# Loading the first query and key blocks of two batches as 2 KB rows and the first weight tiles as fp32 on the same queue, and moving one batch's transposes to DMA

## The chip, the cores and the metric

The kernel runs on one core of one Trainium2 chip. The metric is the device time of one execution, in microseconds (us). Times are medians of several runs. The kernel before the change took 301.33 us (three runs, 300.98 to 301.36). A run counts as slow when it is more than 1.5% above the fastest of its kernel. A point is one per cent of the time before.

## The reference

Two parts follow one another. The first is a sparse attention over 4 batches, 8 heads, 768 tokens and 64 features. Each query picks the 6 best of the 24 chunks of 32 keys by an upper bound, and attends only to these. The second is a gated feed-forward network over the 3072 tokens.

```python
k_min, k_max = min and max of k over each chunk of 32 tokens
ub = np.sum(np.maximum(q * k_min, q * k_max), axis=-1)        # one bound per query and chunk, causal
top_chunks = np.argsort(ub, axis=-1)[..., -6:]
scores = scale * np.matmul(q, k.transpose(0, 1, 3, 2))        # masked to chosen chunks and causal
attn = softmax(scores)
x = (attn @ v) as [3072, 512]                                 # tokens x (heads * features)
gate = np.maximum(x @ w_gate, 0.0)                            # w_gate, w_val: 512 x 1536
out = (gate * (x @ w_val)) @ w_out                            # w_out: 1536 x 512
```

## The kernel before

The first 128 tokens of each batch see only four chunks, so they need no selection. They are done first, as four "first blocks" (one a batch). The other tokens are 16 attention jobs: 4 batches times 4 pairs of heads, job 0 to 3 being batch 0. The feed-forward network runs in six units of 512 tokens and fills TensorE between the attention jobs.

The order of instructions on each engine is not written by hand. Each operation is given to a static list scheduler, called the plan, with an engine, an expected cost in us, a priority (lower goes first) and the things it needs and makes. The plan simulates the kernel from these numbers and fixes one order for each engine. So an edit of a cost or of one load moves many other instructions too.

All plain loads, all transposes that DMA does and all stores are issued by SP, one after the other, in the plan's order. Loads that cast fp32 to bf16 on the way are issued by GpSimd, on another queue.

The loads of a first block, one for each batch and each of q, k, v (256 KB, rows of 64 floats, so 256 bytes):

```python
    def first_block(b):
        ...
                nc.sync.dma_start(out=t[:, 0:H * D].rearrange("p (h d) -> p h d", d=D),
                                  in_=src[b, :, 0:128].rearrange("h p d -> p h d"))
        ...  # then: GpSimd casts to bf16, TensorE transposes, ACT or DVE copies, TensorE scores
```

A transpose is TensorE's or DMA's, by a switch for each batch:

```python
    PE_KQ = lambda b: b < 2          # keys and queries of batches 0 and 1: TensorE
    PE_X = lambda b: b < 2           # attention output of batches 0 and 1: TensorE
    ...
        if on_pe:
            ... nc.tensor.matmul(t[:, r, :], s[:, r, :], ident[0:np_, 0:np_], is_transpose=True, ...)
        else:
            ... nc.sync.dma_start_transpose(out=t, in_=src())
```

The weights come by casting loads from GpSimd, in groups of 2, 3, 3 and 4 column tiles, and a number places the feed-forward work against the jobs:

```python
    WGS = [2, 3, 3, 4]
    ...
                nc.gpsimd.dma_start(out=o, in_=i)          # fp32 in DRAM, bf16 on chip
    ...
            p = 4.0 + HP * (u + done / total)              # priority of feed-forward unit u
```

The softmax here doesn't subtract the row's maximum and nothing guards it: scores larger than these inputs give would overflow.

Of the kernel before, what the change touches and what calls it, by code (L numbers as in the profile page):

```python
# [14 lines left out]
BF16 = mybir.dt.bfloat16  # L15
# [9 lines left out]
class Plan:  # L25
# [8 lines left out]

    LAG = {"PE": 0.38, "ACT": 0.06, "DVE": 0.06, "POOL": 0.06, "SP": 0.06, "DMA": 1.5, "SDMA": 1.7}

    def __init__(self, rings, banks):
        self.rings = rings
        self.banks = banks
        self.ops = []  # L40
        self.made = defaultdict(list)
        self.users = defaultdict(int)
        self.big = set()
# [16 lines left out]
    def share(self, flow, t, events):  # L60

        for s in flow.values():
# [4 lines left out]
            (0.35, 0.65) if flow["DMA"][0] in self.big else (0.21, 0.93))  # L67
# [6 lines left out]
    def order(self):  # L74
# [21 lines left out]
        while len(seq) < n:  # L96
# [13 lines left out]
            for i in ends:  # L110
                o = ops[i]
                for name in [x for _, x in o[5]] + list(o[6]):
                    left[name] -= 1
                for d in outs[i]:
                    need[d] -= 1
                    at[d] = max(at[d], t + (o[7] if ops[d][0] != o[0] else 0.0))
                    if need[d] == 0:
                        wait[ops[d][0]].append(d)
                        heapq.heappush(events, (at[d], -1))
# [40 lines left out]
def kernel(  # L160
# [51 lines left out]
    WIDE = lambda b: b < 1  # L212
    WS = 8
# [3 lines left out]
    PE_KQ = lambda b: b < 2  # L217
    PE_SEL = lambda b: b < 1
    PE_X = lambda b: b < 2
# [5 lines left out]
    WGS = [2, 3, 3, 4]  # L225
# [46 lines left out]
    for nm in "kq":  # L272
        TAGS[f"{nm}bf"] = ([128, 1024], BF16, 2)
        TAGS[f"{nm}0"] = ([128, 512], BF16, 2)
# [15 lines left out]
    rings["dq"] = 6  # L290
    rings["xT"] = XU
    plan = Plan(rings, set(PS))
# [58 lines left out]
    def free_half(j):  # L351
        b, hp = JOBS[j]
        for h in range(2):
# [3 lines left out]
               after=["ind"] + ([("s", j - HP)] if b else []), makes=[("kx0", hp)])  # L357


    def turned(name, tag, src, nr, on_pe, prio, after, makes, hold, np_=128):  # L360
# [10 lines left out]
        else:  # L371
# [3 lines left out]
            dma_t(nr, prio, f, after, makes, take=[(tag, name)], hold=hold)  # L375
# [4 lines left out]
    def dma_t(nr, prio, f, after, makes, take=(), hold=()):  # L380

        made = makes[0]
        op("SP", 1.25, prio, f, after=after, makes=[("ti", made)], take=take, hold=hold, lag=0.0)
        op("DMA", 0.144 * nr, prio, None, after=[("ti", made)], makes=makes,
           hold=list(hold) + [x for _, x in take])
# [18 lines left out]
    def first_block(b):  # L404
        p0 = -30.0 + b
        src3 = (("k", k), ("q", q), ("v", v))
        for nm, src in src3:
            rn = (nm + "raw", "P", b)

            def f_ld(nm=nm, src=src, rn=rn):  # L410
                t = new(nm + "raw", rn)
                nc.sync.dma_start(out=t[:, 0:H * D].rearrange("p (h d) -> p h d", d=D),
                                  in_=src[b, :, 0:128].rearrange("h p d -> p h d"))
            op("SP", 0.6, -40.0 + b + (1.5 if nm == "v" else 0.0), f_ld, makes=[("iss", nm, b - B)],
               take=[(nm + "raw", rn)] + [("dq", ("dq", nm, b - B, i)) for i in range(2)], lag=0.0)
            op("DMA", 1.22, -40.0 + b + (1.5 if nm == "v" else 0.0), None, after=[("iss", nm, b - B)],
               makes=[("ld", nm, b - B)],
               hold=[rn] + [("dq", nm, b - B, i) for i in range(2)])
            if nm == "v":
                op("POOL", 0.61, p0 - 0.1, lambda rn=rn: nc.gpsimd.tensor_copy(  # L420
                    out=v0_l[b % 2][:, :, 0:D],
                    in_=TL[rn][:, 0:H * D].rearrange("p (h d) -> p h d", d=D)),
                    after=[("ld", nm, b - B), ("v00", b % 2), ("av0", b - 2)],
                    makes=[("v", "P", b)], hold=[rn])
                continue
            bn = (nm + "bf", "P", b)

            def f_cast(nm=nm, rn=rn, bn=bn):
                nc.gpsimd.tensor_copy(out=new(nm + "bf", bn)[:, 0:H * D],
                                      in_=TL[rn][:, 0:H * D])  # L430
            op("POOL", 0.61, p0 - 0.2, f_cast, after=[("ld", nm, b - B)], makes=[bn],
               take=[(nm + "bf", bn)], hold=[rn])
            tn, cn = (nm + "T", "P", b), (nm + "0", b)
            tT = turned(tn, "F", lambda bn=bn: TL[bn][:, 0:H * D].rearrange(
                "p (i x) -> p i x", x=128), HP, True, p0, [bn], [tn], [bn])

            def f_c(nm=nm, tT=tT, cn=cn):
                o = new(nm + "0", cn)
                if nm == "q":
                    nc.scalar.activation(out=o, in_=tT(), func=ACT.Copy)  # L440
                else:
                    nc.vector.tensor_copy(out=o, in_=tT())
            op("ACT" if nm == "q" else "DVE", 0.6 if nm == "q" else 0.43, p0, f_c, after=[tn],
               makes=[cn], take=[(nm + "0", cn)], hold=[tn])
        kn, qn, sn, an, xn = ("k0", b), ("q0", b), ("sT", "P", b), ("aT", "P", b), ("x", "P", b)

        def f_s():
            t = new("S", sn)
            for h in range(2):
                nc.tensor.matmul(t[:, h], ident, tri.unsqueeze(1).to_broadcast([128, HP, 128]),  # L450
                                 start=True, stop=False)
            for i in range(HP):
                cs = slice(128 * i, 128 * i + 128)
                for h in range(2):
                    hs = slice(64 * h, 64 * h + 64)
                    nc.tensor.matmul(t[:, h, cs], TL[kn][hs, cs], TL[qn][hs, cs], start=False,
                                     stop=(i == HP - 1))
        op("PE", 0.85, p0, f_s, after=[kn, qn, "tri", "ident"], makes=[sn], take=[("S", sn)],
           hold=[kn, qn])

# [37 lines left out]
    def job_front(j):  # L498
# [4 lines left out]
        wide = WIDE(b)  # L503
# [3 lines left out]
        for nm, src in (("k", k), ("q", q), ("v", v)):  # L507
            rn = (nm + "raw", j)
            big = wide and nm != "v"
# [6 lines left out]
            def f_ld(nm=nm, src=src, rn=rn, np_=np_, ns=ns, lo=lo, big=big):  # L516
# [6 lines left out]
                else:  # L523
                    nc.sync.dma_start(out=o.rearrange("p (h r d) -> p h r d", h=2, d=D),
                                      in_=s.rearrange("h (r p) d -> p h r d", p=128))
            dq = [("dq", nm, j, i) for i in range({"k": 1, "q": 0}[nm] if big else 3)]
            op("SP", 0.6, pL, f_ld, makes=[("iss", nm, j)],
               after=[("iss", x, -1) for x in "kqv"],
               take=[(nm + "raw", rn)] + [("dq", x) for x in dq], lag=0.0)
            i = op("DMA", n * (0.00137 if big else 0.00234), pL, None, after=[("iss", nm, j)],  # L530
                   makes=[("ld", nm, j)], hold=[rn] + dq)
            if big:
                plan.big.add(i)
# [41 lines left out]
        tok = lambda a: a.rearrange("f (p s) -> f p s", s=WS) if wide else a  # L575
# [8 lines left out]
        for m, o in ((0, ALU.min), (1, ALU.max)):  # L584
            def f_mm(m=m, o=o):
                if m == 0:
                    new("kmm", mm)
                if wide:
# [3 lines left out]
                nc.vector.tensor_reduce(out=TL[mm][:, m], in_=i, axis=AX.XY if wide else AX.X,  # L592
# [5 lines left out]
        if PAIR(b):  # L598
            copy_half("DVE", n, pT + 0.05, tok(kx[0]), kT, None,
                      [kn] + [("s", i) for i in prev], [("kx", j)], [kn])  # L600
        for h in range(0 if PAIR(b) else 2):
            copy_half(eng[h], n, pT + 0.05, tok(kx[h][64 * h:64 * h + 64]), kT, h,
# [17 lines left out]
        for nm, e, o in (("qmn", "ACT" if on_pe else "ACT", -1.0),  # L620
                         ("qmx", "ACT" if on_pe else "DVE", 1.0)):
            def f_q(nm=nm, e=e, o=o):
                t = new(nm, (nm, j))
                if e == "ACT":
                    nc.scalar.activation(out=tok(t), in_=qT(), func=ACT.Relu, scale=o)  # L625
# [5 lines left out]
        if PAIR(b):  # L631
            copy_half("ACT", n, pT + 0.06, tok(qx.rearrange("f r h p -> f (r h p)")[:, 0:SQ]), qT,
                      None, [qn, ("s", j - NQX)], [("qx", j)], [qn])

    def job_sel(j):
# [68 lines left out]
        else:  # L704
            dma_t(2 * NQ, p, lambda: nc.sync.dma_start_transpose(
# [67 lines left out]
    def job_av(j, off):  # L773
# [56 lines left out]
        for pi, rs in enumerate(parts):  # L830
# [15 lines left out]
            else:  # L846
                dma_t(len(rs), p, f_xc, aft, mk, take=tk, hold=hd)


    def s1(u, nt, p, wide):  # L850
# [6 lines left out]
        def f_mm(m):  # L857
# [7 lines left out]
            for kt in range(KT_):  # L865
                nc.tensor.matmul(ps, w[:, kt, cs], xT[:, kt, xc:xc + 512], start=(kt == 0),  # L866
                                 stop=(kt == KT_ - 1))
        for m, nm in ((0, gn), (1, vn)):
            op("PE", 0.858, p + 0.001 * m, lambda m=m: f_mm(m),
               after=[xn, ("w", gi)] + ([("g0",) + gn] if m and wide else []),  # L870
               makes=[("d",) + nm] + ([] if m else [("g0",) + gn]),
# [125 lines left out]
```

## Time and profile before

| | before |
|---|---|
| median time, us | 301.33 |
| span of the profiled run, us | 300.6 |
| TensorE busy, us | 273.4 |
| TensorE idle in 0 to 60 / 60 to 200 / after 200 us | 16.3 / 6.6 / 4.3 |

The idle times are the length of a stretch minus the busy time in it. These two lines are from the page of the kernel before: busy time by engine (share of the span, number of instructions), and the chain of work that ended last.

```profile
PE 273.4 (91%) x2258; PEld 145.6 (48%) x2292; DVE 168.3 (56%) x482; ACT 162.5 (54%) x222; POOL 98.0 (33%) x186
...
PE 70%; DMA 18%; DVE 5%; issue 2%; POOL 2%; ACT 1%; SPq 0%; POOLq 0%; ACTq 0%; DVEq 0%
```

TensorE is the bound: busy for 91% of the span. 34 matrix instructions of 2292 have no record in this trace, so its busy time is somewhat more than 273.4 us. The next table is the view of stretches of the same kernel: for each stretch (start and end in us), its length, then busy us of each engine, the clock that TensorE was granted (1.00 is full), the mean busy share of the DMA engines (it adds up the time of all packets, so it can exceed 1) and the rate. The clock has no record before it first went full, at 16.3 us here, and the view shows 1.00 for that time too.

```profile
core 0: us, PE busy (x) PEld busy (x) DVE busy (x) ACT busy (x) POOL busy (x), PEclk, DMA share, GB/s
0.00:60.00 60.00, 43.68 (x443) 24.21 (x449) 39.06 (x118) 28.66 (x38) 32.26 (x56) 0.97 1.20 213
60.00:200.00 140.00, 133.40 (x1350) 77.23 (x1367) 103.08 (x325) 104.06 (x135) 65.29 (x129) 1.00 1.01 176
200.00:320.00 120.00, 96.34 (x473) 44.20 (x479) 26.20 (x40) 29.77 (x50) 0.41 (x1) 0.99 0.09 33
```

60 minus 43.68 is the 16.3 us of idle TensorE in the first stretch; 140 minus 133.40 is 6.6. So there is something to be won in the first 60 us, where the DMA engines are full, and little afterwards. The timeline of GpSimd shows when data comes: each line is start, duration, engine, line of the program, operation, output and input, and in brackets the idle time before it and what ended that.

```profile
4.04 0.61 POOL L429 CAST kbf<-kraw 128x512 bf16<-128x512 f32 x1 [0.97 <-DMA kraw<-in_k_dram]
5.22 0.61 POOL L429 CAST qbf<-qraw 128x512 bf16<-128x512 f32 x1 [0.57 <-DMA qraw<-in_q_dram]
6.43 0.61 POOL L429 CAST kbf<-kraw 128x512 bf16<-128x512 f32 x1 [0.59 <-DMA kraw<-in_k_dram]
7.65 0.61 POOL L429 CAST qbf<-qraw 128x512 bf16<-128x512 f32 x1 [0.61 <-DMA qraw<-in_q_dram]
...
23.02 1.04 POOL L550 CAST kbf<-kraw 96x1024 bf16<-96x1024 f32 x1 [2.16 <-DMA kraw<-in_k_dram]
25.59 1.04 POOL L550 CAST kbf<-kraw 96x1024 bf16<-96x1024 f32 x1 [1.54 <-DMA kraw<-in_k_dram]
```

The first casts start 1.2 us apart, and each waited for its load: 256 KB each 1.2 us is 218 GB/s. The last two are the keys of jobs 0 and 1.

Finally, what TensorE waited for from 60 to 200 us (total, times, longest), the largest item:

```profile
PE sT L741 <- DMA qx_93<-cb_97: 1.8, 1, 1.8
```

These are chosen queries, which DMA transposes for the later batches. TensorE's waits are short here.

### The profile page before, as it was taken

Reading aid. Unit: us, or ns where it says so; the run is one execution under the profiler, and the core shown is the slowest. Engines: PE = TensorE matmul, PEld = TensorE weight load, DVE = VectorE, ACT = ScalarE, POOL = GpSimd, SP = SyncE. Lnnn points to the kernel's source line nnn. Section 1 sums busy time; section 2 is a strip of 40 time slices with the busy share of each in tenths; the row PEclk is TensorE's granted clock in tenths of the full one; section 3 lists DMA queues with packets and bytes.
Section 4 is the critical chain, followed back from the end, with each engine's and each line's share of the span. In section 5 each row is a group of like instructions: output and inputs, shape, how many; then the busy total and the mean of one; then the engine's idle time right before and its main releaser. Section 6 shows DMA issues by size and latency. Waiting matters only on the chain.

```text
span 300.6 us, 5925 instructions
## 1 busy us (share of the span) xinstructions
PE 273.4 (91%) x2258; PEld 145.6 (48%) x2292; DVE 168.3 (56%) x482; ACT 162.5 (54%) x222; POOL 98.0 (33%) x186
## 2 busy tenths in 40 slices
PE   2975796998999999989979899999999999999995
PEld 1542343654665655646545555554444444444441
DVE  4456896759987898978759683204343013103310
ACT  3442494497457868878769867463323223323321
POOL 5674345438644556655644321120000000000000
PEclk9999998999999999999999999999999999999999
DMA  9999999999799999999999622322000020020002
GB/s 168 217 249 215 223 223 227 184 213 221 143 237 234 183 221 204 192 206 188 228 215 236 120 46 44 92 81 59 0 0 0 37 105 0 35 107 0 1 37 106
DMA packets 118269, 41.29 MB, mean 137 GB/s; under 512 B 108128, under 2 KB 113760, under 8 KB 118240
## 3 DMA queue, kind: packets, MB, share of 16 engines
q1 hardware_dynamic: 112448, 36.19, 64.0%
q0 software_dynamic: 5792, 4.72, 9.9%
q8 instruction: 18, 0.29, 0.4%
q14 instruction: 11, 0.09, 0.1%
HBM read 31.20 MB, written 6.29 MB: 125 GB/s over the span
## 4 chain that ended last, share of the span: by engine, by line
PE 70%; DMA 18%; DVE 5%; issue 2%; POOL 2%; ACT 1%; SPq 0%; POOLq 0%; ACTq 0%; DVEq 0%
PE g L866 23%; PE yp L901 19%; PE vl L866 9%; PE sT L741 7%; PE o L793 6%; DMA qraw<-in_q_dram 5%; DMA kraw<-in_k_dram 5%; DMA qx_92<-cb_96 3%; DMA qx_91<-cb_95 3%; DMA qx_93<-cb_97 2%; PE sT L731 2%; DVE hT L885 1%; PE kT L367 1%; PE xt L367 1%; PE ub L651 1%
## 5 line engine op out<-in xcount | busy, mean ns | idle before, releaser
L753 ACT ACTIVATE aT<-sT 128x1024 bf16<-128x1024 f32 x80 | 79.6, 1026 | 23.4 <-PE sT L741 15.7
L877 ACT ACTIVATE grl<-g 128x512 bf16<-128x512 f32 x72 | 43.1, 599 | 57.3 <-PE g L866 57.3
L765 POOL TENSOR_SCALAR_AFFINE_SELECT aT<-aT 128x256 bf16<-128x256 bf16 x80 | 32.3, 418 | 55.7 <-ACT aT L753 47.5
L885 DVE TENSOR_TENSOR hT<-vl,grl 128x512 bf16<-128x512 f32 x48 | 33.0, 688 | 25.2 <-PE vl L866 20.6
L901 PEld LDWEIGHTS <-hT 128*128 128x128 bf16 x288 | 27.4, 98 | 30.6
L885 DVE TENSOR_TENSOR hT<-g,grl 128x512 bf16<-128x512 f32 x24 | 16.6, 692 | 45.2 <-ACT grl L877 29.5
L901 PE MATMUL yp<-wo_70,hT 128*128 128x512 bf16 x141 | 34.8, 379 | 0.2
L592 DVE TENSOR_REDUCE kmm<-kT 128x24 bf16<-128x768 bf16 x32 | 29.6, 946 | 9.0 <-PE kT L367 4.5
L901 PE MATMUL yp<-wo_69,hT 128*128 128x512 bf16 x137 | 34.3, 379 | 0.4
L911 ACT ACTIVATE y<-yp 128x512 f32<-128x512 f32 x24 | 14.3, 596 | 35.0 <-PE yp L901 33.5
L793 PEld LDWEIGHTS <-aT 128*128 128x128 bf16 x640 | 23.7, 99 | 8.2 <-POOL aT L765 2.4
L741 PEld LDWEIGHTS <-kx_all 128*128 128x128 bf16 x192 | 16.0, 98 | 17.8 <-DMA qx_91<-cb_95 2.5
L866 PE MATMUL g<-xT,wg_64 128*128 128x512 bf16 x91 | 24.1, 379 | 0.2
L550 POOL CAST kbf<-kraw 128x768 bf16<-128x768 f32 (+1 forms) x16 | 14.4, 898 | 14.1 <-DMA kraw<-in_k_dram 11.5
L866 PE MATMUL g<-xT,wg_63 128*128 128x512 bf16 x71 | 18.3, 379 | 0.2 <-issue 0.2
L866 PE MATMUL g<-xT,wg_62 128*128 128x512 bf16 x70 | 18.2, 379 | 0.1
L801 DVE RECIPROCAL zr<-o 128x5 f32<-128x5 f32 x32 | 6.1, 190 | 20.5 <-PE o L793 20.5
L808 DVE TENSOR_TENSOR x<-o,zr 128x320 bf16<-128x320 f32 x32 | 15.7, 492 | 1.1
L866 PE MATMUL vl<-xT,wv_68 128*128 128x512 bf16 x61 | 16.1, 379 | 0.2
L550 POOL CAST qbf<-qraw 128x640 bf16<-128x640 f32 (+1 forms) x16 | 13.0, 810 | 9.2 <-DMA qraw<-in_q_dram 9.2
L625 ACT ACTIVATE qmn<-qT 128x640 bf16<-128x640 bf16 x16 | 11.5, 722 | 7.2 <-PE qT L367 6.2
L866 PEld LDWEIGHTS <-wg_64 128*128 128x128 bf16 x96 | 8.9, 98 | 10.7 <-issue 1.3
(178 smaller groups left out, 407.5 us busy)
## 6 DMA issues: line engine op xcount, KB each, us to landing
kraw<-in_k_dram SPq DMA_DIRECT2D x16, 384.0 KB, 6.3
vraw<-in_v_dram SPq DMA_DIRECT2D x16, 384.0 KB, 6.1
out_dram<-y SPq DMA_DIRECT2D x24, 256.0 KB, 2.1
qraw<-in_q_dram SPq DMA_DIRECT2D x12, 384.0 KB, 5.0
qraw<-in_q_dram SPq DMA_DIRECT2D x4, 320.0 KB, 12.3
kraw<-in_k_dram SPq DMA_DIRECT2D x4, 256.0 KB, 4.8
qraw<-in_q_dram SPq DMA_DIRECT2D x4, 256.0 KB, 5.0
vraw<-in_v_dram SPq DMA_DIRECT2D x4, 256.0 KB, 5.1
```

Of the source, the lines that this page charges most:

```text
L550: nc.gpsimd.tensor_copy(out=new(nm + "bf", bn)[0:np_, 0:(ns - r0) * 2 * D].rearrange("p (r h d) -> p r h d", h=2, d=D), in_=TL[rn][0:np_, ...
L592: nc.vector.tensor_reduce(out=TL[mm][:, m], in_=i, axis=AX.XY if wide else AX.X, op=o)
L741: nc.tensor.matmul(t[:, h, o:o + m * 128].rearrange("k (r p) -> k r p", p=128), kx[h][:, c * 128:(c + 1) * 128], qx[:, qb - 1:qb - 1 + m, ...
L753: nc.scalar.activation(out=TL[an][:, :, a0:a0 + w], in_=TL[sn][:, :, 0:w], func=ACT.Exp, scale=scale)
L765: nc.gpsimd.affine_select(out=d, in_=d, compare_op=ALU.is_ge, fill=0.0, base=0, channel_multiplier=-1, pattern=[[0, 2], [1, 128]])
L793: nc.tensor.matmul(TL[on][:, r - 1, h - h0, :], TL[an][:, h, o:o + 128], vb[:, h, c, :], start=(i == 0), stop=(i == NP - 1))
L808: nc.vector.tensor_tensor(out=TL[xn][:, :, h0 * D:(h0 + hs) * D].rearrange("p r (h d) -> p r h d", d=D), in0=TL[on][:, :, :, 0:D], in1=TL[ ...
L866: nc.tensor.matmul(ps, w[:, kt, cs], xT[:, kt, xc:xc + 512], start=(kt == 0), stop=(kt == KT_ - 1))
L877: nc.scalar.activation(out=new("grl", rn), in_=g, func=ACT.Relu)
L885: nc.vector.tensor_tensor(out=TL[hn][:, nt, :], in0=vv, in1=TL[rn], op=ALU.mult)
L901: nc.tensor.matmul(TL[pn], TL[hn][:, nt, tl * 128:(tl + 1) * 128], wo_sb[nt // NPG][:, nt % NPG, :], start=(nt == 0), stop=(nt == NTI - 1))
L911: nc.scalar.activation(out=new("y", yn), in_=TL[pn], func=ACT.Copy)
```

## The change

The intent is to have the first data sooner, and to take work from TensorE, the bound. There are four items, numbered as the prediction numbers them:

1. The first blocks of two batches are loaded together. One load brings half the heads of two batches, and each of its 128 rows is 8 tokens, 2 KB (2 KB in place of 256 bytes). The transposed data are put in order by the copy that follows.
2. The two batches are then cast, transposed and scored together, the query casts move from GpSimd to VectorE, and the matmuls that write the causal mask go ahead of the data.
3. The first four column tiles of both weights (2 MB of fp32) come as plain loads on SP's queue and are cast on chip.
4. The transposes of batch 1 (k, q, x) go from TensorE to DMA.

Besides, many numbers of the plan change: costs, rates, the place of the feed-forward work (4.0 to 1.0), the order of the weight groups. The core of the diff:

```diff
-    PE_KQ = lambda b: b < 2
+    PE_KQ = lambda b: b < 1
     PE_SEL = lambda b: b < 1
-    PE_X = lambda b: b < 2
+    PE_X = lambda b: b < 1
...
-    WGS = [2, 3, 3, 4]
+    WGS = [4, 4, 4]
...
+    def first_front(bp):
+        p0 = -30.0 + 2 * bp
+        for nm, src in (("k", k), ("q", q)):
...
+            def f_ld(nm=nm, src=src, rn=rn):
+                t = new(nm + "raw", rn)
+                s = src[2 * bp:2 * bp + 2, :, 0:128].rearrange(
+                    "b (i h) (p s) d -> h (b i) p (s d)", h=2, s=WS)
+                for h in range(2):
+                    nc.sync.dma_start(out=t[:, h * WS * D:(h + 1) * WS * D], in_=s[h])
+            xfer((nm, 2 * bp - B), 1.1, 1.45, 2, pl, f_ld, makes=[("ld", nm, 2 * bp - B)],
+                 take=[(nm + "raw", rn)], big=True)
...
+    def first_weights():
+        engs = iter(("DVE", "ACT", "POOL", "DVE"))
+        n = 128 * WGS[0]
...
+                    nc.sync.dma_start(out=new(tag, rn)[:, 0:2 * n].rearrange(
+                        "p (k n) -> p k n", n=n), in_=i[:, x:x + 2, 0:n])
+                xfer((nm, "W", x), 0.5, 1.45, 2, -36.0 + 0.1 * m, f_ld, makes=[("ld",) + rn],
+                     take=[(tag, rn)], big=True)
...
-            p = 4.0 + HP * (u + done / total)
+            p = 1.0 + HP * (u + done / total)
```

## The prediction

> **What bounds the kernel now.** The page's busy table gives TensorE 273.4 us of a 300.6 us span (91%); VectorE, ScalarE and GpSimd are at 56, 54 and 33%. In the table of stretches, TensorE is idle 16.3 us of the first 60 us, 7 us from 60 to 200 us (mostly for queries transposed by DMA), about 0.6 us from 200 to 280 us, and 3.9 us at the end (last copy and store). So TensorE work bounds it after about 55 us, and arriving data before. The chain of waits up to 43 us is nearly all loads: query 15.8 to 27.2, key 28.6 to 43.2. DMA share is over 1 there at only 205 to 230 GB/s.
>
> **What the change does, costed.**
> 1. First blocks: eight q/k loads of 256 KB in 256-byte rows become four pairs of 256 KB loads in 2 KB rows. In the timeline the old ones land 1.2 us apart (218 GB/s). The Trainium skill ("DMA: Bandwidth & Descriptors", Specifications) asks for 512 bytes or more for line rate and gives about 358 GB/s as the HBM limit of a core; no part of this trace shows 2 KB rows alone. Estimate from these: 1.45 us per 512 KB, so about 5.8 in place of 9.6 us, 4 us of DMA time saved.
> 2. Two batches are cast, transposed and scored at once; half of the casts move from GpSimd to VectorE. The first mask matmuls (1.04 us a pair, slow clock) move ahead of the data, where TensorE is idle.
> 3. The first four column tiles of both weights (2 MB of fp32) come over SP's queue, 2 KB rows, and cost four casts (0.7 to 1.05 us) on three engines. Before, the casting GpSimd loads landed 5 to 20 us after issue; wv_65 held TensorE until 25.2 us, wv_66 until 32.3. They are now 4 MB, not 6 MB, beside the SP loads.
> 4. Batch 1's k, q and x transposes leave TensorE for DMA: 64 transposes (by the order of instructions). A group of six takes 0.51 us against 0.22 for one, so 0.058 us each: 3.7 us. In return some 24 more DMA transposes (about 8 us of DMA time, estimated) fall at 60 to 110 us, where the DMA share is already 0.8 to 1.4.
>
> **On the critical path.** Item 4's 3.7 us counts fully: TensorE is nearly saturated there and feed-forward matmuls fill waits. Of the 4 to 5 us of DMA time from 1 and 3, I expect 3 to 4 us as less TensorE idle before 60 us; part goes to a later first feed-forward matmul (it waits for 2 MB of plain loads, beside the casting queue from about 12 us). From 60 to 200 us I give back about 1 us to later DMA transposes. Sum: 301.3 - 3.7 - 3.5 + 1 = about 295.
>
> Predicted: **295.0 us**, 8 in 10 within 289.5 to 299.5. Faster by over 2%: 0.52; within 2%: 0.46; slower: 0.02.
>
> **What would show it.** TensorE busy about 269 to 270 us. Idle before 60 us about 12 to 13 us, from 16.3. First-block q/k landing about 1.5 us per 512 KB. First feed-forward matmul at 20 to 26 us, then no weight waits over 1 us. Job 0's bound matmuls (29.7 us before) at 26 to 33 us. Idle 60 to 200 us at 7 to 9 us.
>
> **What would make it wrong.** The casting queue starving SP's plain weight loads, so that feed-forward starts after 30 us: no gain there, about 298. Or DMA transposes of batch 1 delaying scores by several us. Conversely, if early feed-forward fills every wait, idle before 60 us falls below 9 us and the time to 290.

## More of the kernel before

The timeline of SP shows how it issues (L521 is a load of keys or queries of batch 0, in long rows; x2 is two loads):

```profile
16.29 0.39 SPq L521 DMA_DIRECT2D kraw<-in_k_dram  x1
...
17.27 11.23 SPq L521 DMA_DIRECT2D qraw<-in_q_dram  x2
```

Of these 11.23 us for two issues one took 10.6, and a load of values later took 11.6. SP was then not waiting for data; it stood in the issue itself, while earlier transfers were still being worked off. What stands behind such a load in SP's order waits with it.

## The result, and the profile after

| | before | after |
|---|---|---|
| median time, us (four runs each, same chip) | 301.35 | 317.97 |
| lowest to highest | 300.98 to 302.06 | 316.26 to 318.40 |
| TensorE busy, us | 273.4 | 278.5 |
| TensorE idle in 0 to 60 / 60 to 200 / after 200 us | 16.3 / 6.6 / 4.3 | 21.8 / 11.6 / 3.9 |

The ratio of after to before is 1.0538 (95% interval 1.0493 to 1.0583): slower by more than 5%. A ratio here is the mean time of one kernel's fast runs over the mean of the other's of the same rounds, so it is not quite the ratio of the medians quoted. All ratios below are to the kernel before, run on the same chip in the same rounds.

The page of after, the same two lines:

```profile
PE 278.5 (88%) x2228; PEld 145.1 (46%) x2228; DVE 164.6 (52%) x476; ACT 164.5 (52%) x221; POOL 93.2 (30%) x177
...
PE 44%; DMA 7%; ACT 1%; issue 1%; DVE 0%; POOL 0%; ACTq 0%; POOLq 0%
```

The stretches of after:

```profile
0.00:60.00 60.00, 38.16 (x271) 19.57 (x271) 28.86 (x80) 19.82 (x26) 21.72 (x35) 0.94 0.98 210
60.00:200.00 140.00, 128.36 (x1264) 70.66 (x1263) 101.49 (x318) 96.81 (x127) 63.54 (x122) 0.99 1.10 188
200.00:320.00 120.00, 111.94 (x697) 54.86 (x694) 34.20 (x80) 47.89 (x70) 7.93 (x20) 0.99 0.15 46
```

TensorE's idle time grew by 5.5 us in the first stretch and by 5.0 in the second, and its busy time by 5.1. With 0.4 us less at the end, that accounts for the 15.2 us of span. The growth of busy time is partly a gap in the records of before (34 missing; after has none of its 2228 missing), partly slow clock, as shown further down, so it can't be split exactly. The same gap makes the idle time of before look somewhat longer than it was.

First, when data come. The casts of the key pairs of the first blocks are on GpSimd, and of the query pairs on VectorE; the two later lines of the first fence are the keys of jobs 0 and 1.

```profile
6.45 1.04 POOL L440 CAST kbf<-kraw 128x1024 bf16<-128x1024 f32 x1 [3.39 <-DMA kraw<-in_k_dram]
...
15.35 1.04 POOL L440 CAST kbf<-kraw 128x1024 bf16<-128x1024 f32 x1 [2.15 <-DMA kraw<-in_k_dram]
...
35.96 1.04 POOL L579 CAST kbf<-kraw 96x1024 bf16<-96x1024 f32 x1 [3.33 <-DMA kraw<-in_k_dram]
...
49.22 1.04 POOL L579 CAST kbf<-kraw 96x1024 bf16<-96x1024 f32 x1 [1.67 <-DMA kraw<-in_k_dram]
```

```profile
10.50 0.69 DVE L442 CAST qbf<-qraw 128x1024 bf16<-128x1024 f32 x1 [6.36 <-DMA qraw<-in_q_dram]
...
19.20 0.69 DVE L442 CAST qbf<-qraw 128x1024 bf16<-128x1024 f32 x1 [6.87 <-DMA qraw<-in_q_dram]
```

Before, the last cast of k0, q0, k1 and q1 began at 7.65 us; now the last cast of the same four (one k pair and one q pair) begins at 10.50. The keys of job 0 come at 35.96 in place of 23.02 us, those of job 1 at 49.22 in place of 25.59. What loads did meanwhile is seen in the view of stretches, before and then after:

```profile
4.00:6.00 2.00, 0.72 (x6) 0.46 (x7) 0.57 (x2) 0.00 (x0) 1.22 (x2) 1.00 1.37 219
...
8.00:10.00 2.00, 1.70 (x14) 0.69 (x12) 0.23 (x1) 0.80 (x1) 0.88 (x2) 1.00 1.39 218
```

```profile
4.00:6.00 2.00, 0.98 (x3) 0.07 (x1) 0.15 (x1) 0.00 (x0) 0.00 (x0) 1.00 0.57 212
...
8.00:10.00 2.00, 0.58 (x6) 0.31 (x3) 0.00 (x0) 0.00 (x0) 0.00 (x0) 1.00 0.83 157
```

The DMA engines are not full: their mean share is 0.57 and 0.83 where it was 1.37 and 1.39, and from 8 to 10 us they move 157 GB/s where it was 218. From 4 to 6 us a share of 0.57 moved nearly what 1.37 had moved: long rows do take less engine time for a byte. But part of the engines has nothing to do. Then SP's order in after (L966 loads the fp32 weights, L556 the keys of jobs 0, 1, ...):

```profile
12.49 1.70 SPq L966 DMA_DIRECT2D kraw<-in_moe_w_gate_dram  x1
...
16.03 3.03 SPq L966 DMA_DIRECT2D kraw<-in_moe_w_val_dram  x1
...
21.09 0.41 SPq L556 DMA_DIRECT2D kraw<-in_k_dram  x1
...
24.63 9.99 SPq L556 DMA_DIRECT2D kraw<-in_k_dram  x1
```

The weight loads stand ahead of the keys of job 0 (issued at 21.09, in before from 14.5 us on), and the keys of job 1 stood 10 us in the issue. The first feed-forward matmuls, in TensorE's timeline:

```profile
33.01 1.87 PE L895 MATMUL g<-xT,wg_61 128*128 128x512 bf16 x4 [0.52 <-DVE xT L529]
...
38.05 1.03 PE L895 MATMUL vl<-xT,wv_64 128*128 128x512 bf16 x4
```

Feed-forward begins at 33.0 us (21.5 before), and cold: the same four matmuls take 1.87 us, and 1.03 us from 38.05 on. The clock has its first record, at full, at 38.0 us (16.3 in before). Idle TensorE costs a second time in this way. The stretches around two later gaps show it (the column after POOL's is the clock):

```profile
48.00:51.70 3.70, 1.76 (x16) 0.58 (x13) 1.47 (x2) 0.88 (x2) 1.28 (x2) 0.99 1.19 235
51.70:58.50 6.80, 5.95 (x31) 2.22 (x32) 3.74 (x7) 3.55 (x5) 5.04 (x7) 0.50 0.87 155
120.00:123.30 3.30, 0.78 (x4) 0.41 (x5) 0.41 (x1) 0.97 (x2) 1.06 (x3) 1.00 0.99 172
123.30:126.70 3.40, 3.40 (x21) 1.62 (x19) 0.40 (x1) 1.54 (x2) 0.49 (x2) 0.51 0.84 162
```

After a stretch in which TensorE was busy 1.76 of 3.7 us the clock was half for 6.8 us, and after one with 0.78 of 3.3 us for 3.4 us. Together 10.2 us at half clock, against 3.4 us in before. The Trainium skill ("TensorE: Matmul & The Clock Gate", "Part 1: The HAM clock gate (the "warmup" mystery)", "What's actually happening") says that the clock falls to half after an idle window of about 3.4 us and comes back after as long a busy one. This agrees in the size of the step (0.50 and 0.51 granted) and in the length (3.4 us, and twice that). But TensorE was not wholly idle ahead of either: low use was enough in these two. From 167.7 to 171.1 us it was busy only 1.62 of 3.4 us as well, and the clock stayed full, so where the limit lies is not shown.

From 60 to 200 us the largest wait of TensorE is again for queries transposed by DMA, and longer:

```profile
PE sT L770 <- DMA qx_90<-cb_94: 5.2, 2, 2.7
```

### The profile page after: what moved, and what is told of

It is laid out like the page before. It is cut to its first block, busy times and chain, and to the rows that moved or that the text cites. A ratio compares the mean times of both kernels' runs of the same rounds, so it can differ in the third digit from the quotient of the medians.

```text
span 315.8 us, 5854 instructions
## 1 busy us (share of the span) xinstructions
PE 278.5 (88%) x2228; PEld 145.1 (46%) x2228; DVE 164.6 (52%) x476; ACT 164.5 (52%) x221; POOL 93.2 (30%) x177
## 4 chain that ended last, share of the span: by engine, by line
PE 44%; DMA 7%; ACT 1%; issue 1%; DVE 0%; POOL 0%; ACTq 0%; POOLq 0%
PE g L895 18%; PE yp L932 13%; PE vl L895 6%; DMA kT<-kbf 5%; PE sT L770 4%; PE o L822 2%; DMA qx_90<-cb_94 2%; PE ub L680 0%; ACT aT L782 0%; ACT y L942 0%; POOL aT L794 0%; ACT kx_all L402 0%; DVE hT L916 0%; DVE x L837 0%; DVE zr L830 0%
## 5 line engine op out<-in xcount | busy, mean ns | idle before, releaser
L782 ACT ACTIVATE aT<-sT 128x1024 bf16<-128x1024 f32 x80 | 79.8, 1023 | 23.9 <-PE sT L770 17.1
L932 PE MATMUL yp<-wo_68,hT 128*128 128x512 bf16 x144 | 35.0, 379 | 0.0
L932 PE MATMUL yp<-wo_67,hT 128*128 128x512 bf16 x144 | 35.0, 379 | 0.0
L895 PE MATMUL g<-xT,wg_61 128*128 128x512 bf16 x96 | 26.4, 399 | 0.5 <-DVE xT L529 0.5
L770 PEld LDWEIGHTS <-kx_all 128*128 128x128 bf16 x192 | 16.3, 98 | 22.2 <-DMA qx_90<-cb_94 5.8
L895 PE MATMUL g<-xT,wg_62 128*128 128x512 bf16 x96 | 25.6, 391 | 0.0
L895 PE MATMUL g<-xT,wg_63 128*128 128x512 bf16 x96 | 24.6, 379 | 0.5 <-ACT grl L908 0.5
L895 PE MATMUL vl<-xT,wv_65 128*128 128x512 bf16 x64 | 18.2, 410 | 0.0
L895 PE MATMUL vl<-xT,wv_66 128*128 128x512 bf16 x64 | 16.4, 379 | 1.6 <-DVE hT L916 1.6
L895 PE MATMUL vl<-xT,wv_64 128*128 128x512 bf16 x64 | 17.3, 394 | 0.0
L402 ACT ACTIVATE kx_all<-kT 64x768 bf16<-64x768 bf16 x12 | 10.0, 835 | 11.4 <-DMA kT<-kbf 11.4
L770 PE MATMUL sT<-qx_90,kx_all 128*128 128x512 bf16 (+3 forms) x64 | 11.2, 299 | 5.2 <-DMA qx_90<-cb_94 5.2
```

Source lines behind the costliest of these rows:

```text
L770: nc.tensor.matmul(t[:, h, o:o + m * 128].rearrange("k (r p) -> k r p", p=128), kx[h][:, c * 128:(c + 1) * 128], qx[:, qb - 1:qb - 1 + m, ...
L782: nc.scalar.activation(out=TL[an][:, :, a0:a0 + w], in_=TL[sn][:, :, 0:w], func=ACT.Exp, scale=scale)
L895: nc.tensor.matmul(ps, w[:, kt, cs], xT[:, kt, xc:xc + 512], start=(kt == 0), stop=(kt == KT_ - 1))
L932: nc.tensor.matmul(TL[pn], TL[hn][:, nt, tl * 128:(tl + 1) * 128], wo_sb[nt // NPG][:, nt % NPG, :], start=(nt == 0), stop=(nt == NTI - 1))
```

## The experiments

Eighteen kernels ran. All gave the reference's result but the probe. Where a text names a theory by a letter, the heading or the text beside it says what is tested. Most edits of a kernel also change the plan's order, and the group at the end asks how much that alone is worth. The exception is 8 against 16 engines (after and e2, e3 and e6, e18 and e7): that edit touches only access patterns, and in the traces of all three pairs SP and TensorE have the same operations in the same order.

### A. The eight loads that use eight DMA engines

The Trainium skill ("DMA: Bandwidth & Descriptors", "Why a DMA increments its semaphore by 16 and not by 1") says that a DMA is spread over k engines, where k is the largest number up to 16 that divides the slowest dimension (of a size other than 1) of both its access patterns, and that with loads issued by SP only those k engines post a completion. Here that is 8 for the source (2 batches x 4 heads). The trace agrees: each paired load left 8 completion packets of four bytes, every other load 16. The rival was that the rate of 2 KB rows was simply over-estimated.

**e1_probe**: a kernel of its own (wrong result) loads 256 KB of keys one at a time, each followed by one VectorE instruction that waits for it.

```diff
+ a: k[2*bp:2*bp+2, :, 0:128].rearrange("b (i h) (p s) d -> h (b i) p (s d)", h=2, s=8)   # as in after: slowest 8
+ b: k[2*bp:2*bp+2, :, 0:128].rearrange("b (i h) (p s) d -> h p (b i) (s d)", h=2, s=8)   # same bytes: slowest 16
+ c: k[b, :, 0:128].rearrange("h p d -> p h d")                                           # as before: 256-byte rows, 128
+ d: as a, but each batch by itself: two loads of 128 KB, slowest 4
```

> A probe with a wrong output on purpose: loads of the first blocks one at a time, each waiting for the one before. Theory A (the slowest dimension of the new source pattern is 8, so each new load uses only 8 of the 16 DMA engines): form a (as in the changed kernel, 256 KB, 2 KB rows, slowest dimension 8) takes about 1.3 us longer in data than one with 16 engines would: from the 200 GB/s seen in the changed kernel at 3 to 6 us, 256 KB need 1.3 us, form b (slowest dimension 16, same bytes) about 0.7 us, form d (slowest dimension 4) about 1.3 us as its two halves of 4 engines do not spread either, or 2.6 us if both use the same 4; form c (256-byte rows, 16 engines) 1.2 us. In issue-to-landing time: a 0.6 us above b, a about equal to c. Rival B (the 2 KB rows are fast and the start is slow because of the load of weights on the same queue and beside it): a and b land alike, both well before c.

In the timeline of VectorE, the bracket is the time from the end of the instruction before (when the next load is issued) to the landing; ta to td are the forms a to d.

```profile
9.75 0.69 DVE L37 TENSOR_TENSOR acc<-acc,ta 128x512 f32<-128x512 f32 x1 [4.04 <-DMA ta<-in_k_dram]
...
18.25 0.69 DVE L37 TENSOR_TENSOR acc<-acc,tb 128x512 f32<-128x512 f32 x1 [3.61 <-DMA tb<-in_k_dram]
...
25.65 0.69 DVE L37 TENSOR_TENSOR acc<-acc,tc 128x512 f32<-128x512 f32 x1 [3.10 <-DMA tc<-in_k_dram]
31.80 0.69 DVE L37 TENSOR_TENSOR acc<-acc,td 128x512 f32<-128x512 f32 x1 [5.46 <-DMA td<-in_k_dram]
```

Form a took 4.0 to 4.1 us (without the first load, whose bracket starts later than its issue), b 3.5 to 3.6, c 2.9 to 3.1, d 5.3 to 5.5 (issue and fixed latency included). From first to last packet of a load it was about 2.0 us for a and 1.3 us for b. So sixteen engines in place of eight save about 0.7 us of data time on one load, and 0.5 us to its landing. The other half was a surprise: the old rows of 256 bytes landed *sooner* than 2 KB rows on all 16 engines. The Specifications table of the same page gives 512 bytes as the smallest transfer for line rate, on which the prediction rested; one load of this size does not show that.

**e2_k16**: after, with the same bytes in an order whose slowest dimension is 16.

```diff
-                    "b (i h) (p s) d -> h (b i) p (s d)", h=2, s=WS)
+                    "b (i h) (p s) d -> h p (b i) (s d)", h=2, s=WS)
...
-                i = TL[tn].rearrange("f s (b x) -> f b x s", b=2)
+                i = TL[tn].rearrange("f s (p b i) -> f b i p s", b=2, i=HP)
```

> The changed kernel with only the partition order of the paired loads turned, so that their slowest dimension is 16 (and the copies after the transposes read it back in the new order). Theory A: first q pair's cast at about 6 us in place of 10.5, second q pair's at about 11 in place of 19.2; first feed-forward matmul at about 25 us in place of 33; total time about 303 us, in place of 318, if the later idle time is a consequence of the late start; 310 or more if it is not. Rival B (contention with weights): under 3 us gained in total.

313.80 us, ratio 1.0436 (1.0381 to 1.0491): about 1 point of the 5.4 comes back. The key pairs (GpSimd) and the first query pair (VectorE) are cast at

```profile
5.65 1.04 POOL L440 CAST kbf<-kraw 128x1024 bf16<-128x1024 f32 x1 [2.59 <-DMA kraw<-in_k_dram]
...
12.46 1.04 POOL L440 CAST kbf<-kraw 128x1024 bf16<-128x1024 f32 x1 [1.50 <-DMA kraw<-in_k_dram]
```

```profile
7.90 0.69 DVE L442 CAST qbf<-qraw 128x1024 bf16<-128x1024 f32 x1 [3.76 <-DMA qraw<-in_q_dram]
```

in place of 6.45, 15.35 and 10.50 us. So the first two pairs are 2.25 us apart on 16 engines and 4.05 on 8; the prediction had priced 1.45. 512 KB each 2.25 us is 233 GB/s, little more than the 218 of the old rows. From 12 to 20 us, with many loads in flight, 281 GB/s are moved (239 in after, 234 in before). The first feed-forward matmul is at 26.3 in place of 33.0 us. But most of the time that this won ahead is lost again at the next obstacle. SP, in e2:

```profile
18.98 12.36 SPq L556 DMA_DIRECT2D kraw<-in_k_dram  x1
```

The keys of job 1 stood 12.4 us in the issue, and were cast at 41.1 us (49.2 in after, 25.6 before). The mechanism is shown; its worth alone is small as long as the rest is in place.

### B. The fp32 weights on SP's queue, and the transposes of batch 1

**e3_pe2**: after, with item 4 taken back. **e4_sw0**: after, with item 3 taken back (the first weight group again as two casting loads of GpSimd).

```diff
-    PE_KQ = lambda b: b < 1
+    PE_KQ = lambda b: b < 2
-    PE_X = lambda b: b < 1
+    PE_X = lambda b: b < 2
```

```diff
-    first_weights()
...
+            if w == 0:
+                weight(("w" + nm, 0), o, x[:, :, cs], 0.88 * n, -28.5, [("iss","v",-1)], 1.5)
```

> The changed kernel with batch 1's transposes back on TensorE. Theory A with a late start that the static order never makes good: start unchanged (first feed-forward matmul at 33 us), total within 3 us of 318. Rival C (the DMA transposes of batch 1 delay the attention and so make the 11 us of TensorE idle at 120 to 190 us): last exp 15 us or more earlier than 236.9 us, idle 60 to 200 us back to about 7 us, total 308 to 312.

> The changed kernel with the first four column tiles of both weights again as casting loads by GpSimd. Theory A: first q pair still cast at about 10.5 us and the second at 17 to 19 us, total within 4 us of 318. Rival B (plain weight loads on SP's queue make the start late): first feed-forward matmul before 27 us and total under 310.

e3: 313.23 us, 1.0393 (1.0337 to 1.0449); one of its four runs, 316.43 us, was slow and is not in the ratio. TensorE's idle time from 60 to 200 us fell to 7.5 us, as Rival C said, but the last exponential of the attention came only about 3 us earlier, not 15. e4: 314.33 us, 1.0476 (1.0418 to 1.0533); this interval overlaps that of after, so its 0.6 points are not clear of noise. No item alone brings back more than 1.5 points. Then both together with A:

> Both repairs: loads over 16 engines and batch 1's transposes on TensorE. If the two losses are separate and add (4 us each), about 309 us; idle before 60 us about 17.5 us as in e2, idle 60 to 200 us about 7.5 us as in e3. If the second only hid behind the first: 313 or no better than each alone.

> Both repairs, and the first weights cast by GpSimd's loads again. If the fp32 weights on SP's queue, ahead of job 0's k and q, are the third loss: job 0's first exp before 41 us and total 303 to 306 us. If they are not (contention is the same wherever the weights come from): within 2 us of e6.

e6 (16 engines, item 4 undone): 308.83 us, 1.0224 (1.0167 to 1.0281). e7 (16 engines, items 4 and 3 undone): 301.70 us, 0.9992 (0.9953 to 1.0032). With all three mended the loss is gone. What remains of the change in e7, pairing two batches, the earlier masks and the plan's numbers, gains nothing measurable.

**e18_pe2_sw0**: e7, but with the loads of item 1 on eight engines as in after.

> e7 without its repair of the loads: batch 1's transposes and the first weights as in the kernel before, but the paired loads with slowest dimension 8. If 8 engines instead of 16 are worth about as much here as alone (e2: 4 us) or with one other repair: 305 to 308 us, first exp at about 14 us and job 0's first exp 5 us or more later than e7's 38.3 us.

311.83 us, 1.0340 (1.0296 to 1.0384): more than the 305 to 308 us expected. The six kernels and after, as ratios to before:

| | slowest 8, fp32 weights on SP | slowest 16, fp32 weights on SP | slowest 8, weights by GpSimd | slowest 16, weights by GpSimd |
|---|---|---|---|---|
| batch 1's transposes on DMA | 1.0538 (after) | 1.0436 (e2) | 1.0476 (e4) | not run |
| on TensorE | 1.0393 (e3) | 1.0224 (e6) | 1.0340 (e18) | 0.9992 (e7) |

Read the lower row. Going from 8 to 16 engines is worth 1.7 points with the weights on SP (e3 to e6) and 3.5 without (e18 to e7). Taking the weights off SP is worth 0.5 points with 8 engines (e3 to e18, not clear of noise) and 2.3 with 16 (e6 to e7). Read down the columns: item 4 costs 1.4 to 2.1 points in each of the three pairs, whatever the order. The keys of jobs 0 and 1 show the two early faults: they are cast at 20.8 and 25.0 us in e7, at 32.2 and 42.3 with the weights on SP (e6), at 33.2 and 36.9 on 8 engines (e18). Each fault hides part of the other: the early stage waits for whatever comes last, and mending one leaves the other. That is why single undoing showed so little. The stretch 0 to 60 us of e18, then the first two of e7:

```profile
0.00:60.00 60.00, 39.38 (x319) 20.77 (x320) 31.91 (x91) 24.16 (x32) 23.77 (x40) 0.86 1.00 203
```

```profile
0.00:60.00 60.00, 49.08 (x485) 26.48 (x486) 42.60 (x120) 31.63 (x42) 28.38 (x49) 0.97 1.13 224
60.00:200.00 140.00, 129.25 (x1245) 73.08 (x1241) 96.40 (x304) 94.10 (x125) 61.11 (x120) 1.00 0.93 170
```

TensorE is idle 20.6 us in the first in e18 and 10.9 in e7. It also ran slower in e18: the clock was half for 17.1 us from 22.4 us on (0.86 over the stretch, 0.97 in e7). So once the faults are gone, early idle time falls below before's 16.3 us, and below the 12 to 13 us that the prediction forecast. It had put this down to faster rows, which e1 does not show for one load; what part of the change does it was not isolated. e7 gives that back from 60 to 200 us: 10.75 us idle, against 6.6 in before. What causes this later idle time in e7 was not isolated; the plan's order differs there throughout.

### C. What the DMA transposes of batch 1 cost, in the kernel before

**e5_before_pe1**: before, with item 4 alone. **e12_before_kq1**: only its keys and queries.

```diff
-    PE_KQ = lambda b: b < 2
+    PE_KQ = lambda b: b < 1
-    PE_X = lambda b: b < 2         (e5 only)
+    PE_X = lambda b: b < 1
```

> The kernel before with item 4 of the prediction alone: batch 1's k, q and x transposes moved from TensorE to DMA. The prediction costed this at -3.7 us of TensorE work and +1 us of waits, so 298 to 299 us against 301. Rival C (the DMA transposes in that stretch cost more than they save, as e3 suggests, where putting them back gained 4 us): same or slower, 300 to 306 us, with 3 to 5 us more TensorE idle at 60 to 200 us.

> The kernel before with batch 1's k and q transposes on DMA, and its x transposes left on TensorE (half of e5). Occupancy: about half to two thirds of e5's loss, 304 to 306 us. If the x transposes (which gate the feed-forward of unit 2) are the loss: within 1% of 301.

e5: 309.00 us, 1.0227 (1.0172 to 1.0283). Item 4, which was to win 3.7 us, costs 7 by itself. e12: 301.35 us, 0.9997 (0.9960 to 1.0034), neutral. (The profiled run of e12 was its slowest, 304.34 us.) So the net loss seems to come with the transposes of x, which feed the feed-forward network; 8 transposes more on SP, 52 against 44. But both orders differ too. TensorE's stretch from 60 to 200 us in e5:

```profile
60.00:200.00 140.00, 124.17 (x1213) 68.39 (x1210) 98.45 (x313) 97.97 (x127) 63.03 (x123) 1.00 1.11 186
```

It is idle 15.8 us of 140 (6.6 in before), and this increase of 9.2 us is about the increase of the span (309.2 less 300.6, 8.6 us). SP's timeline in e5 shows one candidate for the cause (L374: DMA transposes of k and q of a job; L524 and L521: loads; L915: a store):

```profile
82.07 1.25 SPq L524 DMA_DIRECT2D qraw<-in_q_dram  x1
83.42 2.36 SPq L374 DMA_TRANSPOSE kT<-kbf  x1
85.88 2.10 SPq L374 DMA_TRANSPOSE qT<-qbf  x1
88.06 0.53 SPq L915 DMA_DIRECT2D out_dram<-y  x1
88.65 0.42 SPq L524 DMA_DIRECT2D vraw<-in_v_dram  x1
```

SP has about 0.1 us between one issue and the next here; its queue is full. A plain load costs it 0.42 to 1.25 us in these lines, a DMA transpose 2.10 to 2.36 us. Over the whole of before, 36 DMA transposes took 1.2 us at least and 1.5 at the median (1.8 on average), and plain loads and stores 0.6 us at the median (loads alone 0.8). From 60 to 200 us SP is issuing for 101 us in before, 121 in e5 and 120 in after. The last load is issued at 161 us in before, 179 in e5 and 176 in after, and the last exponential of the attention starts at 199.5, 209.2 and 236.9 us (with feed-forward at 1.0 in after, which also moves it).

The rivals: is it the bytes of the transposes on the DMA engines, or SP's issuing time (which includes standing in the issue)? Three kernels add useless work to before, at the places where batch 1's keys and queries are ready, and take nothing from TensorE.

**e11_before_dummy**: 8 useless DMA transposes.

```diff
+        if b == 1:
+            for nm in "kq":
+                turned((nm + "D", j), "tT", bf(nm), geo[nm][1], False, pT + 0.01, [(nm + "bf", j)], ...)
```

> The kernel before, with TensorE's transposes of batch 1 kept, and the 8 DMA transposes of k and q of batch 1 added beside them into tiles that nothing reads (the output stays right). TensorE's work is unchanged. If the DMA queue has room there, time stays within 1% of 301. If occupancy of the one full queue is the loss in e5 (there: 9 us more idle from 24 transposes, 8 of k and q, 8 of x), then 4 to 8 us slower, 305 to 309, though no instruction waits for these transposes to land except those that reuse their buffers. If the loss in e5 is only the latency of the chain (cast, transposes, copies), no loss here.

**e13_before_dumload**: 8 useless plain loads of as many bytes (196 KB each). **e14_before_dumtiny**: 24 useless loads of 512 bytes.

```diff
+                nc.sync.dma_start(out=t.bitcast(FP32), in_=moe_w_gate[128 * hp:128 * hp + 128, 0:384])   (e13)
+                nc.sync.dma_start(out=new("xd", dn), in_=moe_w_gate[0:128, z:z + 1])                    (e14)
```

> As e11, but the 8 useless DMA transposes (196 KB each for k) are 8 useless plain loads of the same 196 KB, in rows of 1.5 KB, into the same ring of tiles and at the same place of the plan. In e11 a transpose held SP's queue for 1.2 us at least and 1.9 us in the mean, while a plain load holds it some 0.6 us. If SP's time for issuing is the full resource at 80 to 160 us (18.2 to 18.9 of each 20 us are taken in the kernel before and in e5): at most a third of e11's loss, under 2 us. If the DMA engines are (their share is over 1): 4 us or more.

> The kernel before with 24 useless loads of 4 bytes a partition (512 bytes each) for batch 1, 6 for each job. They add nearly no bytes. SP's time: 24 issues of about 0.4 to 0.5 us, some 10 us in all, about as e11 added (9.3 us). If SP's time for issuing is the resource: 3 to 6 us slower. If the DMA engines' bytes are: within 1%.

e11: 306.74 us, 1.0191 (1.0162 to 1.0220). e13: 297.88 us, 0.9875 (0.9820 to 0.9930). e14: 309.65 us, 1.0280 (1.0216 to 1.0343). The same bytes as plain loads do not slow the kernel, and 12 KB in 24 pieces slow it most. So a loss does not need the bytes, and the bytes alone did not make one. The DMA engines' share from 60 to 200 us was 1.09, 1.03 and 0.95 (1.01 in before), not in the order of the three times. SP's issuing time in that stretch was 110.6, 102.0 and 112.3 us (101.3 in before), which is in that order. That fits SP's time as the cause and does not prove it: e13 issues 8 loads more at nearly the same sum, so the sum is also a result of how long SP stood, e14 had 13.7 us at half clock (3.4 in before), and all three orders differ. That e13 came out *faster* than before has no cause but the plan's order, as far as any run shows.

But the sum of SP's time is not the whole of it: e12 has 112.8 us and lost nothing (it saves TensorE an estimated 2.5 us: 44 transposes at 0.058 us). Two kernels with all stores issued by ScalarE in place of SP tested this further:

```diff
-        op("SP", 0.5, p, lambda: nc.sync.dma_start(out=out[r0:r0 + 128, :], in_=TL[yn]),
+        op("ACT", 0.1, p - 20.0, lambda: nc.scalar.dma_start(out=out[r0:r0 + 128, :], in_=TL[yn]),
```

> e10 (the kernel before with 1.0 for 4.0) with the 24 stores of the output issued by ScalarE right after the copy that makes them, in place of SP. About 9 of them stand on SP's queue before 160 us. If SP's time is the resource: 1 to 4 us faster than e10, 295 to 297 us. If not: within 1 us of e10, or slower as ScalarE pays for the issues.

> e5 (the kernel before with all of batch 1's transposes on DMA, SP full at 18.4 to 18.9 of each 20 us from 80 to 180 us) with the stores issued by ScalarE. If SP's time is the resource: 2 to 5 us faster than e5, 304 to 307 us. If not: within 1.5 us of e5's 309.

e15 (on e10, see D): 298.60 us, 0.9891 (0.9826 to 0.9956); its profiled run, 302.20 us, slow, is not in the ratio. Against e10's 0.9914 there is no gain. e16 (on e5): 306.99 us, 1.0178 (1.0119 to 1.0237), against e5's 1.0227; the intervals overlap, so it is inconclusive, though SP's sum fell from 120.6 to 112.2 us. The Trainium skill ("DMA: Bandwidth & Descriptors", "Issuing engines are not separate DMA queues") says that issuing from several engines saves only the sequencer's time to initiate a DMA, "which is usually small relative to the DMA itself". For one load that holds here: 0.6 us at the median, against 5 to 6 us to landing for most loads of before. But the sum is not small: SP was in an issue for 101 of 140 us in before, standing in it included. But e15 gives no sign that moving the stores would win it back.

**e17_e7_x3**: the other direction, e7 with the transposes of x of batch 2 on TensorE too (`PE_X = lambda b: b < 3`).

> e7 with batch 2's x transposes on TensorE too: 4 DMA transposes fewer (5 to 7 us of SP's queue), 20 TensorE transposes more (1.2 us). In e7 SP is taken 17 to 19 of each 20 us from 60 to 140 us and TensorE idles 10.7 us at 60 to 200 us. If SP's queue is what makes that idle time: idle there falls by 3 us or more and the total is 298 to 300.5. If not: 1 us slower than e7's 301.7, or a mere change of order, within 3 us either way.

303.35 us, 1.0035 (0.9990 to 1.0080), six runs, one of which took 1587 us and is the profiled one (slow, not in the ratio), so there is no profile to read. If SP's time in transposes of x were all, this should have won; it did not.

### D. What the plan's numbers alone do

Theory D: after tells the plan 1.45 us for 512 KB, the loads take longer, and the order is bad because of it. **e8_k16_pe2_cost** is e6 with the measured cost. Theory E: it is the place of the feed-forward work, 4.0 in before and 1.0 in after. **e9_e7_prio4** is e7 with 4.0, **e10_before_prio1** is before with 1.0.

```diff
-            xfer((nm, 2 * bp - B), 1.1, 1.45, 2, pl, f_ld, ...          (e8, and so for the weights)
+            xfer((nm, 2 * bp - B), 1.1, 2.2, 2, pl, f_ld, ...
-            p = 1.0 + HP * (u + done / total)                           (e9; e10 the other way round)
+            p = 4.0 + HP * (u + done / total)
```

> As e6, but the static plan is told 2.2 us for each 512 KB load of 2 KB rows in place of 1.45 us; it then orders v of job 0 after k and q of jobs 1 and 2. Theory D (the rest of the loss is an order of instructions built on loads that are too fast, with v of job 0 in 256-byte rows ahead of job 1's k and q in the one queue): job 1's first exp, 60 us in e2, comes before 52 us, and total is 3 us or more below e6. Otherwise within 2 us of e6.

> e7 with the feed-forward work's place in the plan as in the kernel before (4.0 in place of 1.0). e7 has 5 us less idle before 60 us than the kernel before (10.9 against 16.3) and 4 us more at 60 to 200 us (10.7 against 6.6). Theory E (feed-forward taken 3 places earlier runs out at 100 to 160 us, so waits there are bare): idle at 60 to 200 us back to about 7 us, idle before 60 us up to 12 us, total 296 to 299. Otherwise within 2 us of 301.7, or slower.

> The kernel before with that number alone changed (1.0 in place of 4.0). Theory E: idle at 60 to 200 us rises by 2 to 4 us, total 302 to 305. If the place is neutral: within 1% of 301.

e8: 317.32 us, 1.0499 (1.0443 to 1.0555), 8.5 us slower than e6. A truer cost made the order worse; Theory D fell. e9: 305.33 us, 1.0133 (1.0105 to 1.0160), slower than e7; its early idle time is 10.6 us, so what was won early does not come from the feed-forward's place. e10: 298.46 us, 0.9914 (0.9891 to 0.9937), faster than before. 1.0 is the better place in both kernels, so Theory E fell too. TensorE's idle time in e10 is 14.2 us in the first 60 us and 4.5 from 60 to 200, against 16.3 and 6.6 in before. e10 beats both kernels: 0.9% less than before, about 6% less than after. It is one number of the change, taken alone. And since e7 has this place too and e9, with before's place, is at 1.0133, the paired front and the other numbers of the plan have paid nothing in e7; at this size the plan's order could still hide a gain or a loss.

This group also gives the noise of the method. Edits of nothing but the plan's numbers moved the time by -2.6 (e10), +4.2 (e9, by the ratios) and +8.5 us (e8). A single difference of up to 8.5 us between two kernels of different order can therefore be the order and not the thing edited. Every single difference in C, but for e14's 9.0 us, lies within this, and so do e4's and the 7.1 us from e6 to e7. The steps from 8 to 16 engines are free of it, as the order is the same; item 4 rests on four pairs of the same sign (after and e3, e2 and e6, e4 and e18, e5 and before: 1.4 to 2.3 points).

## Why the prediction was wrong

Predicted 295.0 us (289.5 to 299.5); measured 317.97. The direction was wrong, and slower had been given 0.02. Point by point:

- *"So TensorE work bounds it after about 55 us, and arriving data before."* Right for before. It holds less in after, where TensorE is idle 11.6 of the 140 us from 60 to 200 us: the losses are 5.5 us of early idle time, 5.0 us of later idle time and a longer busy time.
- *Item 1, "1.45 us per 512 KB, so about 5.8 in place of 9.6 us, 4 us of DMA time saved."* This is the step that failed first. The first two pairs of after came 4.05 us apart (6.45, 10.50) where 1.45 was priced. Eight engines explain 1.8 us of that; on sixteen they came 2.25 us apart (e2), so the priced rate was too high even then. The prediction read the row length from the pattern and not the slowest dimension, which also was there to be read, and no trace had shown 2 KB rows at the rate that it took. Spreading the loads over 16 engines is worth 1.0 point alone (e2), and 3.5 with the other faults gone (e18 to e7). Even on 16 engines a 2 KB load did not land sooner than the old one (3.5 against 3.0 us in e1), and e7 with 16 engines is level with before. So "3 to 4 us as less TensorE idle" had the wrong sign in after: 5.5 us more.
- *Item 2.* Masks ahead of the data, casts shared: they happened, and with the faults gone early idle time is 10.9 us (e7), less than before. That the total still shows no gain was not foreseen.
- *Item 3, "They are now 4 MB, not 6 MB, beside the SP loads."* It counted bytes on the casting queue and not places in SP's queue. 2 MB went ahead of the keys of jobs 0 and 1. In the prediction's sum it had no cost except "part goes to a later first feed-forward matmul". Measured: 0.6 points, an estimated 1.9 us and not clear of noise, if it alone is undone (e4), and 7.1 us at the end of the chain (e6 308.83, e7 301.70, same chip), change of order included.
- *Item 4, "3.7 us counts fully" and "give back about 1 us".* The gain can't be read from before and after, because records of before are missing. In pairs with all records TensorE was busy 276.3 with item 4 and 279.7 without (e2, e6), 276.0 and 277.7 (e4, e18), 278.5 and 278.2 (after, e3), slow clock included: at most 3.4 us less. The give-back was mis-sized: alone in before item 4 makes the kernel 7 us slower (e5, order included), so what it cost was over 7 us, not 1. It was priced as "about 8 us of DMA time", but as many bytes as eight of these transposes, as plain loads, cost nothing (e13). There were 16 more DMA transposes, not 24 (52 against 36), and each holds SP for 1.2 us or more, which the prediction did not price.
- *"The casting queue starving SP's plain weight loads, so that feed-forward starts after 30 us: no gain there, about 298."* Feed-forward started at 33.0 us, so this risk came true, by another mechanism in part (slow first loads, and the queue's order). It was sized at +3 us. The late start also left TensorE cold until 38.0 us.
- *Slower clock* was in no term. After had 10.2 us of recorded half clock, before 3.4; half of the difference, an estimated 3.4 us, is the most that TensorE work can have lost by it. The cold start comes on top: ahead of the first record of a full clock TensorE was busy 19.2 us in after (to 38.0 us) and 9.8 in before (to 16.3 us), and half of that difference is 4.7 us, an estimate of the most again.

**What stays open.** Whether, and why, the transposes of x and not those of k and q carry the net loss of e5: SP's issuing time fits e5, e11, e13 and e14, but not e12 (neutral at 112.8 us), e17 (no gain) and e15 (no gain). It is a supported reason and not a settled one; the order in which SP takes them, waiting for x in its queue, was not separated from the time that they take. And the share of the plan's order in each single ratio is not known.

## What to carry to other kernels

Read the slowest dimension of a load's pattern before the length of its rows: a rearrangement that makes rows longer can halve the number of DMA engines, and the DMA share in a stretch shows it. A queue that is issued in order has two prices, bytes and places: ask what stands behind each new transfer, and what its issue costs the issuing engine. When several faults sit in one early stage, undo them together and in pairs; each alone looked like 0.6 to 1.5 points, and together they were the whole 5.4.

## What the Trainium skill lacked or had wrong

- "DMA: Bandwidth & Descriptors", Specifications, smallest transfer for line rate: for a single 256 KB load, 256-byte rows on 16 engines landed in 2.9 to 3.1 us and 2 KB rows on 16 engines in 3.5 to 3.6 us (e1). The page does not say that the gain of longer rows is not seen in the latency of one load of this size, and successive 512 KB pairs of 2 KB rows moved at 233 GB/s (e2).
- The same page, "Why a DMA increments its semaphore by 16 and not by 1": the rule for k was right (8 completion packets, and 16). It gives no price: here 4.0 against 3.5 us for one load, and up to 3.5% of the kernel (e18 against e7).
- The same page, "DMA Transpose (X-bar)": no time, measured on this chip, that a DMA transpose takes of the sequencer that issues it (the page has cycle counts for "previous generations" only in a table about a later chip). Here 1.2 us at least and 1.5 us at the median (before, 36 of them), against 0.6 us for plain loads and stores.
- The same page, "Issuing engines are not separate DMA queues": the sequencer's time to issue is called usually small beside the DMA itself. True here of one load (0.6 us, 5 to 6 us to landing); not said is that the sum can fill the sequencer: SP was in an issue for 101 of the 140 us from 60 to 200 us in before, and for 121 in e5.
- "TensorE: Matmul & The Clock Gate", Part 1: the clock is said to fall after an idle window, and in a later passage after frequent short gaps; how low the use must be is not given. Here it fell to half after 3.7 us in which TensorE was busy 1.76 us, and after 3.3 us with 0.78 us busy, but not after 3.4 us with 1.62 us busy (after).
- No page has it: an issue by SP took up to 11.6 us (before) and 12.4 us (e2) while earlier transfers were worked off, and everything behind it in SP's order stood with it.
